# Values of the last six token tiles, two tiles at a time

## The chip, the cores and the metric

One core of a Trainium2 chip. The metric is the device time of one execution in microseconds (us); lower is better. TensorE (PE) multiplies matrices into PSUM, VectorE (DVE) and ScalarE (ACT) work on PSUM and SBUF, GpSimd (POOL) on SBUF, SyncE (SP) issues most DMAs. The engines run side by side; each takes its own instructions in the order in which they are written.

## The reference

A gated block: linear attention with a learned feature map, times a gated MLP, plus the input. There are 2048 tokens of width 640, 32 heads of 20 and a hidden width of 1536; all is float32.

```python
def _A_ref(x, wqkv, w_phi, wo):
    qkv = (x @ wqkv).reshape(B, S, 3, H, Dh).transpose(2, 0, 3, 1, 4)
    q, k, v = qkv[0], qkv[1], qkv[2]
    pq = jnp.einsum("bhsd,hdf->bhsf", q, w_phi)
    pk = jnp.einsum("bhsd,hdf->bhsf", k, w_phi)
    phi_q = jnp.concatenate([_softmax(pq), _softmax(-pq)], axis=-1)
    phi_k = jnp.concatenate([_softmax(pk), _softmax(-pk)], axis=-1)
    kv = jnp.einsum("bhsf,bhsd->bhfd", phi_k, v)
    z  = jnp.einsum("bhsf->bhf", phi_k)
    num = jnp.einsum("bhqf,bhfd->bhqd", phi_q, kv)
    den = jnp.einsum("bhqf,bhf->bhq", phi_q, z)[..., None] + 1e-6
    return (num / den).transpose(0, 2, 1, 3).reshape(B, S, D) @ wo
xn = _layernorm(x)
s = _A_ref(xn, A_wqkv, A_w_phi, A_wo)
g = _silu(_gelu(xn @ B_w1 + B_b1) @ B_w2 + B_b2)
return x + s * g
```

## The kernel before

The tokens are 16 tiles of 128; tiles 2q and 2q+1 form pair q. In the first phase each tile's normalized input, transposed and stationary, is multiplied with the weights of key, value and query (w_phi is folded into those of key and query). Every operand is split into a high and a low half, and three products of halves (`PASSES`) are summed. So `project` (L363) issues, for each of five blocks of the width, three passes of two matmuls of 128x320: 30 for one projection of one tile. Their sum lies in a PSUM bank of the pool `pA`, of which there are three.

What follows a key or a query is `feat1` and `feat2`. VectorE takes the maximum and the minimum of each head (`mx` L376, `mn` L377), subtracts the maximum (`e` L380, the last reader of the bank) and forms `nr` (L383); GpSimd makes the other half of the features from `nr` and `e` (L384, called `rest` here); ScalarE takes exp (L393). `nr` has two buffers. For a key, VectorE sums each head (L401), takes the reciprocal (L426), and GpSimd scales (`scale_heads`, L406); queries are stored to DRAM (`e_dram`) from ScalarE. `value` copies its bank into a row with ones between the heads, and two GpSimd memsets set those (L413, L414). `kv_pair` adds two tiles' products of keys and values, 64 small matmuls each, to a bank of its own.

A pair's input `xr` is prepared by `pair_stats` (mean and spread, a power on GpSimd at L231, a small store to `st_dram` and a broadcast load `bc`), `pair_sub` (GpSimd, L332), `pair_mul` (VectorE, L337) and `pair_plain` (high halves on ScalarE, L283, low halves on VectorE, L285). `t_sums` (GpSimd, five subtractions at L298) and `t_split` (ScalarE L314, GpSimd L315) make `xd`, sums of blocks of the two tiles. They serve Strassen's product in the variant with seven products: queries of pairs 4 to 7 are made by `query_pair`, both tiles at once, in seven parts of 6 or 9 matmuls, 54 for two tiles where `project` needs 60. The parts' sums, X, Y, V, Z and W, are brought together on ScalarE, GpSimd and VectorE. For this the weights' sums S1 to S4 are needed too; `fold_pair`, `s_hi` and `s_lo` make those of the query weights at tiles 4 and 5, store them to `s_dram`, and `s_back` loads them at the end. The MLP's first product uses the same `xp` and `xd`.

The order is written by hand throughout the first phase: the order of the calls in the loops over the tiles is the order on each engine. From tile 6 on a tile's step is key, value, and for tiles 6 to 9 two queries of earlier tiles; then key and value alone up to tile 15, then the four query pairs, and the MLP.

## Time and profile before

| | us |
|---|---|
| median of 3 executions | 656.03 (655.87 to 656.10) |
| the profiled execution | 655.47 |
| its span, first to last instruction | 653.8 |

The profile is of one execution, which took 655.47 us, 0.56 below the median. A share such as PE's is busy time over the span; a line such as L363 is one of the listing above. In the chain of work that ended last, each row gives start, length, engine, tile and line, and in the waits an engine's idle time is put down to what ended it. The first phase ends at about 243 us; the rest is the MLP and the attention's output.

### The profile page before, as it was taken

To read this page: it belongs to the slowest core of one execution; us is meant where nothing else is said; L and a number is where in the kernel's file an instruction comes from. 1 tells how busy PE (TensorE), PEld (TensorE's weight loads), DVE (VectorE), ACT (ScalarE), POOL (GpSimd) and SP (SyncE) were. 2 spreads that over 40 slices of the span, in tenths; PEclk is the share of its full clock that TensorE was granted. 3 is DMA by queue.
4 is the path that set the end of the run, shared out by engine and by line. 5 is a ranking of instruction groups with operands and counts; after the bars stand their busy time and mean duration, and the time that the engine had idled before them with its cause. 6 is when DMAs were issued, how large, how long until landed. Compare 5 with 4: busy or idle time off the path is not lost.

```text
span 653.8 us, 11408 instructions
## 1 busy us (share of the span) xinstructions
PE 648.0 (99%) x4414; PEld 563.0 (86%) x4414; DVE 476.0 (73%) x749; ACT 235.3 (36%) x334; POOL 389.5 (60%) x348
## 2 busy tenths in 40 slices
PE   9999999999999999999999999999999999999997
PEld 9999999999999998888888888888888886766866
DVE  6785956988655887578978967858889899852232
ACT  4512513333233357153343355742231524032130
POOL 2755464949669655867778776354462967343321
PEclk9999999999999999999999999999999999999999
DMA  9706083664204487355998899596969499989962
GB/s 351 277 1 168 12 308 133 154 181 137 84 2 162 148 286 253 121 159 203 260 257 287 230 421 290 94 335 224 171 219 259 66 270 192 301 219 260 286 228 81
DMA packets 161408, 132.22 MB, mean 202 GB/s; under 512 B 89170, under 2 KB 127314, under 8 KB 160458
## 3 DMA queue, kind: packets, MB, share of 16 engines
q1 hardware_dynamic: 158618, 119.89, 63.0%
q10 hardware_dynamic: 2736, 11.60, 4.9%
q8 instruction: 35, 0.57, 0.4%
q14 instruction: 19, 0.16, 0.1%
HBM read 83.74 MB, written 47.73 MB: 201 GB/s over the span
## 4 chain that ended last, share of the span: by engine, by line
PE 76%; DVE 3%; DMA 0%; issue 0%; POOL 0%; ACT 0%; DVEq 0%; SPq 0%; ACTq 0%
PE pB L812 24%; PE pB L783 22%; PE pB L967 11%; PE pA L363 10%; PE pA L616 4%; PE pB L914 2%; PE kv L435 1%; PE qV L616 1%; DVE y L821 1%; PE pB L921 1%; PE qY L616 1%; DMA phi_t<-eq 0%; POOL e L384 0%; DVE nr L383 0%; DVE wolh L891 0%
## 5 line engine op out<-in xcount | busy, mean ns | idle before, releaser
L812 PE MATMUL pB<-hs,w2s 128*128 128x512 f32 x720 | 165.8, 389 | 0.0
L812 PEld LDWEIGHTS pB<-hs,w2s 128*128 128x128 f32 x720 | 135.0, 188 | 28.8 <-DVE y L821 0.8
L783 PE MATMUL pB<-xp,w1s 128*128 128x512 f32 x324 | 81.4, 389 | 0.0
L783 PE MATMUL pB<-xd,w1s 128*128 128x512 f32 x324 | 79.3, 389 | 0.0
L967 PE MATMUL pB<-oT,wo 128*128 128x512 f32 (+1 forms) x315 | 72.3, 381 | 0.0
L783 PEld LDWEIGHTS pB<-xd,w1s 128*128 128x128 f32 x324 | 60.8, 188 | 12.6
L783 PEld LDWEIGHTS pB<-xp,w1s 128*128 128x128 f32 x324 | 60.7, 188 | 12.7 <-DVE pB L1048 0.2
L406 POOL TENSOR_TENSOR eq<-eq,rc 128x1280 f32<-128x1280 f32 x16 | 37.9, 2372 | 54.2 <-DVE rc L871 37.1
L967 PEld LDWEIGHTS pB<-oT,wo 128*128 128x128 f32 x315 | 57.2, 188 | 13.8 <-PE pB L914 2.5
L406 POOL TENSOR_TENSOR e<-e,rc 128x1280 f32<-128x1280 f32 x16 | 37.9, 2368 | 45.9 <-DVE rc L426 45.6
L821 DVE TENSOR_TENSOR y<-pB,y 128x512 f32<-128x512 f32 x100 | 63.1, 676 | 1.4 <-PE pB L812 1.4
L393 ACT ACTIVATE e<-e 128x1280 f32<-128x1280 f32 x32 | 40.7, 1272 | 64.4 <-POOL e L384 63.5
L788 ACT ACTIVATE pB<-pB,b1t 128x512 f32<-128x512 f32 x48 | 31.8, 662 | 78.8 <-DVE pB L1048 28.9
L363 PE MATMUL pA<-wv,xp 128*128 128x320 f32 x384 | 59.8, 310 | 0.1
L363 PE MATMUL pA<-wk,xp 128*128 128x320 f32 x384 | 59.6, 310 | 0.0
L363 PEld LDWEIGHTS pA<-wv,xp 128*128 128x128 f32 x384 | 56.9, 188 | 0.4 <-DVE e L380 0.4
L384 POOL TENSOR_TENSOR e<-nr,e 128x640 f32<-128x640 f32 x32 | 43.8, 1371 | 22.4 <-DVE nr L383 19.3
L363 PEld LDWEIGHTS pA<-wk,xp 128*128 128x128 f32 x384 | 56.9, 188 | 0.1
L858 POOL TENSOR_TENSOR ez<-eq,zrep 128x1280 f32<-128x1280 f32 x16 | 47.3, 2958 | 2.5 <-DMA eq<-e_dram 2.5
L463 POOL TENSOR_TENSOR w1s<-raw,w1s 128x640 fp32r<-128x640 f32 (+1 forms) x18 | 26.2, 1457 | 30.6 <-ACT w1s L462 30.6
L401 DVE TENSOR_REDUCE rc<-e 128x64 f32<-128x1280 f32 x16 | 23.7, 1482 | 18.4 <-ACT e L393 18.3
L970 POOL TENSOR_TENSOR xres<-gt,xres 128x256 f32<-128x256 f32 x20 | 14.3, 737 | 36.2 <-DVE gt L969 36.2
(165 smaller groups left out, 1090.2 us busy)
## 6 DMA issues: line engine op xcount, KB each, us to landing
raw<-in_w_dram SPq DMA_DIRECT2D x42, 320.0 KB
e_dram<-e ACTq DMA_DIRECT2D x16, 640.0 KB
eq<-e_dram SPq DMA_DIRECT2D x16, 640.0 KB
phi_t<-eq SPq DMA_DIRECT2D x64, 160.0 KB
phT<-phi_t SPq DMA_DIRECT2D x20, 480.0 KB
xres<-in_xt_dram SPq DMA_DIRECT2D x20, 256.0 KB
xt<-in_x_dram SPq DMA_DIRECT2D x15, 320.0 KB
out_dram<-xres SPq DMA_DIRECT2D x18, 256.0 KB
```

The source lines that it names most:

```text
L363: nc.tensor.matmul(ps[:, hf, :HALF], stat_x(q, o, k, a), ws[k][:, b, hf * HALF:(hf + 1) * HALF], start=n == 0, stop=n == 3 * KC - 1)
L384: rest = lambda: nc.gpsimd.tensor_tensor(e5[:, :, :, 1, :], nr[:, :, :, None].to_broadcast([P, 2, 16, DH]), e5[:, :, :, 0, :], op=OP.subtract)
L393: nc.scalar.activation(ef, ef, AF.Exp)
L406: nc.gpsimd.tensor_tensor(e3, e3, rc[:, :, None].to_broadcast([P, 64, DH]), op=OP.mult)
L463: nc.gpsimd.tensor_tensor(sl[:, 1, :n], src, sl[:, 0, :n].bitcast(F32), op=OP.subtract)
L616: nc.tensor.matmul(bank[ch], q_x(blk, a, q), q_weight(w, k)[:, b], start=ch not in seen and n == 0, stop=n == len(mms) - 1, skip_group_che ...
L783: nc.tensor.matmul(bank[ch][:], tl[:, a, off + wo_:off + wo_ + P], mov(blk, b), start=new and n == 0, stop=n == len(mms) - 1, skip_group_c ...
L788: nc.scalar.activation(ps, ps, AF.Gelu_apprx_tanh, bias=b1t[:, f:f + 1])
L812: nc.tensor.matmul(ps[:], ws[i][:, b, d * P:(d + 1) * P], hs[o][i][:, a, :], start=i == n == 0, stop=(i, n) == (GF - 1, 2), skip_group_che ...
L821: nc.vector.tensor_tensor(y, ps[:], y, op=OP.add)
L858: nc.gpsimd.tensor_tensor(zv, ef, zf, op=OP.mult)
L967: nc.tensor.matmul(ps[:, mv], w, o[:, mv], start=n == 0, stop=n == 15, skip_group_check=True)
```

## The change

The values of tiles 10 to 15 are no longer projected tile by tile but by pairs, with the routine of the query pairs (now `token_pair`, with the base weights and the forms handed in). The forms S1 to S4 of the value weights are made by `v_forms` from reloaded weights, for i = 0 on GpSimd at tile 5, for i = 1 on VectorE at tile 8, go through `sv_dram`, and are split by `forms` when pair 5 is at hand: high halves on ScalarE, low halves on VectorE. The query weights' sums are now stored unsplit (`sq_dram`) and split in the same way in the last pair, and the lower halves of two query slabs go through `wq_dram`. `t_sums` works in place in `xr`, and the blocks of `xd` have another order, so that `reload` has nine loads rather than eight. The steps from tile 6 to 9 prepare one pair each; then follow pairs 5 to 7, each with its two keys, a `kv_pair` and the value pair, and last the query pairs. The warm-up's ten matmuls go to one bank.

In the diff the loop that is taken out is left away; it is in the listing above.

```diff
-    s_dram = dram.tile([4, P, 2, D], F32, name="s_dram")
+    sv_dram = dram.tile([4, P, D], F32, name="sv_dram")
+    sq_dram = dram.tile([4, P, D], F32, name="sq_dram")
+    wq_dram = dram.tile([2, P, 2, HALF], F32, name="wq_dram")
...
-        return [(i, a), (2 + i, b)]
-
-    def s_hi(pairs):
-        out = []
-        for k, r in pairs:
-            hi = row([P, D], F32R, "sh")
-            nc.scalar.activation(hi[:], r[:], AF.Copy)
-            out.append((k, r, hi))
-        return out
-
-    def s_lo(parts):
-        for k, r, hi in parts:
-            nc.gpsimd.tensor_tensor(r[:].bitcast(F32R), r[:], hi[:].bitcast(F32), op=OP.subtract)
-            nc.sync.dma_start(s_dram[k][:, 0], hi[:].bitcast(F32))
-            nc.sync.dma_start(s_dram[k][:, 1], r[:])
+        nc.sync.dma_start(sq_dram[i], a[:])
+        nc.sync.dma_start(sq_dram[2 + i], b[:])
+
+    def w_dump(c):
+        nc.sync.dma_start(wq_dram[c], wq_s[c][:, :, :HALF].bitcast(F32))
+
+    def v_forms(i):
+        a, b = (load_raw(wv[c * P:(c + 1) * P, :]) for c in (i, 2 + i))
+        yield
+        eng = nc.vector if i else nc.gpsimd
+        put = lambda d, x, y, op: eng.tensor_tensor(d, x, y, op=op)
+        put(b[:, HALF:], a[:, HALF:], b[:, HALF:], OP.add)
+        put(a[:, HALF:], a[:, :HALF], a[:, HALF:], OP.subtract)
+        put(a[:, :HALF], b[:, HALF:], a[:, :HALF], OP.subtract)
+        put(b[:, :HALF], b[:, :HALF], a[:, :HALF], OP.subtract)
+        nc.sync.dma_start(sv_dram[i], a[:])
+        nc.sync.dma_start(sv_dram[2 + i], b[:])
+        yield
...
     def t_sums(q):
-        xr = xrs.pop(q)
-        tts[q] = slab(F32, "tt", (P, 9, P))
-        x_sums(lambda a, b: xr[:, a:b, :P], lambda a, b: xr[:, a:b, P:], tts[q])
+        xr = xrs[q]
+        x_sums(lambda a, b: xr[:, a:b, :P], lambda a, b: xr[:, a:b, P:],
+               lambda t: xt_two(xr.rearrange("p k (o t) -> p (k o) t", o=2), t))
 
     def t_split(q):
-        tt, dst = tts.pop(q), xd()[:, :, :, at(q)]
-        nc.scalar.activation(dst[:, :, 0, :], tt[:], AF.Copy)
-        nc.gpsimd.tensor_tensor(dst[:, :, 1, :], tt[:], dst[:, :, 0, :].bitcast(F32), op=OP.subtract)
+        dst = xd()[:, :, :, at(q)]
+        tt = xrs.pop(q).rearrange("p k (o t) -> p (k o) t", o=2)[:, :9]
+        nc.scalar.activation(dst[:, :, 0, :], tt, AF.Copy)
+        nc.gpsimd.tensor_tensor(dst[:, :, 1, :], tt, dst[:, :, 0, :].bitcast(F32), op=OP.subtract)
...
-    for pw in (bankA(), bankA()):
-        for i in range(5):
+    for pw in (bankA(),):
+        for i in range(10):
...
+    vf = [v_forms(0), v_forms(1)]
     for t in range(2, 6):
         pk = project(t, wk_s)
         if t % 2:
             kv_pair(t - 3)
         es[t] = feat1(pk)
+        if t == 4:
+            next(vf[0])
...
-            if t == 5:
-                s_lo(s_hi(srs[0]))
-            srs.append(fold_pair(t - 4))
+            fold_pair(t - 4)
+        if t == 5:
+            next(vf[0])
         feat2(es[t])
         if t == 4:
             pair_plain(3)
         phis[t] = key_fin(es.pop(t))
-        if t == 5:
-            s_lo(s_hi(srs[1]))
-    def s_back():
+    def q_back(c):
+        sl = slab(F32R, "wqb")
+        wq_b.append(sl)
+        nc.sync.dma_start(sl[:, :, :HALF].bitcast(F32), wq_dram[c])
+
+    def split_to(dst, src, eng):
+        nc.scalar.activation(dst[:, 0], src, AF.Copy)
+        eng.tensor_tensor(dst[:, 1], src, dst[:, 0].bitcast(F32), op=OP.subtract)
+
+    def forms(dram, f, base, engs):
+        raws = [load_raw(dram[k]) for k in range(4)]
+        yield
         for k in range(4):
-            sl = slab(F32R, "wqs")
-            nc.sync.dma_start(sl[:].bitcast(F32), s_dram[k])
-            wq_f.append(sl)
+            if k < 3:
+                f.append(slab(F32R, "ws"))
+            if k < 2:
+                split_to(f[k][:], raws[k][:], engs[k])
+            else:
+                split_to(base[k - 2][:, :, HALF:], raws[k][:, HALF:], engs[k])
+                split_to(f[2][:, :, (k - 2) * HALF:(k - 1) * HALF], raws[k][:, :HALF], engs[k])
+            yield
...
-    def query_pair(q, hooks, later):
+    def token_pair(q, base, f, hooks, later=None, out=None):
...
+            elif i == 2 and out:
+                nc.scalar.activation(out[0][:, 0], heads1(bank["X"]), AF.Copy)
             elif i == 3:
                 nc.vector.tensor_tensor(r2[:, 1], r2[:, 0], bank["V"], op=OP.add)
             elif i == 4:
-                nc.vector.tensor_tensor(odd[:, 1, :HALF], r2[:, 1], bank["Z"], op=OP.add)
+                o = out[1][:, 1] if out else heads1(odd[:, 1, :HALF])
+                nc.vector.tensor_tensor(o, heads1(r2[:, 1]), heads1(bank["Z"]), op=OP.add)
             elif i == 5:
-                nc.vector.tensor_tensor(bank["W"], r2[:, 1], bank["W"], op=OP.add)
-                ee = feat1(even)
+                o = out[0][:, 1] if out else heads1(bank["W"])
+                nc.vector.tensor_tensor(o, heads1(r2[:, 1]), heads1(bank["W"]), op=OP.add)
+                ee = None if out else feat1(even)
             elif i == 6:
-                nc.vector.tensor_tensor(bank["Z"], r2[:, 0], bank["Z"], op=OP.add)
+                o = out[1][:, 0] if out else heads1(bank["Z"])
+                nc.vector.tensor_tensor(o, heads1(r2[:, 0]), heads1(bank["Z"]), op=OP.add)
             if i in hooks:
                 hooks[i]()
-        return ee, feat1(odd, later)
+        return (ee, feat1(odd, later)) if not out else None
+
+    def value_pair(q, hooks):
+        vv = [value_row() for _ in range(2)]
+        token_pair(q, wv_s, wv_f, hooks, None, [v3[:, :, :DH].rearrange("p (a h) d -> p a h d", a=2) for _, v3 in vv])
+        vs[2 * q], vs[2 * q + 1] = (v for v, _ in vv)
...
+    XIN = {6: (12, 13), 8: (14, 15)}
+    STATS = {6: (10, 11), 7: (12, 13), 9: (14, 15)}
+    x_in(10)
+    x_in(11)
+    for t in range(6, 10):
+        q = t - 2
         pk = project(t, wk_s)
+        if t == 8:
+            kv_pair(6)
+        if t == 9:
+            vb = forms(sv_dram, wv_f, wv_s, [nc.vector] * 4)
+            next(vb)
+        if t == 6:
+            spill(3)
+        es[t] = feat1(pk)
+        if t > 6:
+            pair_plain(q - 1)
+        if t < 9:
+            pair_sub(q)
+        if t == 6:
+            fold_w(wqT, range(4, KC), "wq", wq_s)
+        if t < 8:
+            load_xr(q + 1)
+        feat2(es[t])
+        vs[t] = value(t)
+        phis[t] = key_fin(es.pop(t))
+        if t > 6:
+            t_sums(q - 1)
+        pq = project(next(queries), wq_s)
+        ef = feat1(pq)
+        if t < 9:
+            pair_mul(q)
+        if t in (7, 8):
+            next(vf[1])
+        for u in STATS.get(t, ()):
+            pair_stats(u)
+        store_e(queries_done.pop(0), ef)
+        pq = project(next(queries), wq_s)
+        ef = feat1(pq)
+        if t > 6:
+            t_split(q - 1)
+        store_e(queries_done.pop(0), ef)
+        if t == 6:
+            kv_pair(4)
+        if t in (6, 7):
+            w_dump(t - 6)
         for u in XIN.get(t, ()):
             x_in(u)
+    qf, later, last_sums = None, [], []
+    for p in range(5, 8):
+        t = 2 * p
+        pk = project(t, wk_s)
+        if p == 7:
+            w1r = load_w1(0)
+            qf = forms(sq_dram, wq_f, wq_b, [nc.vector] * 4)
+            next(qf)
         es[t] = feat1(pk)
+        if p == 5:
+            load_xr(7)
+            next(vb)
+            next(vb)
+        if p == 6:
+            pair_mul(7)
+        pk = project(t + 1, wk_s)
+        kv_pair(t - 2)
+        es[t + 1] = feat1(pk, later)
+        if p == 7:
+            next(qf)
+            next(qf)
+            q_back(0)
+            q_back(1)
+            wq_b.extend(wq_s[2:])
+        if p == 6:
+            pair_plain(7)
+
+        def rest(t=t, p=p):
+            later.pop(0)()
             feat2(es[t])
+            if p == 5:
+                next(vb)
+            if p == 6:
+                t_sums(7)
+            if p == 7:
+                next(qf)
+
+        def first_key(t=t, p=p):
             phis[t] = key_fin(es.pop(t))
+            feat2(es[t + 1])
+
+        def second_key(t=t, p=p):
+            if p < 7:
+                phis[t + 1] = key_fin(es.pop(t + 1))
+            else:
+                phis[t + 1] = es.pop(t + 1)
+                last_sums.append(key_sums(phis[t + 1]))
+            if p == 5:
+                pair_sub(7)
+            if p == 6:
+                t_split(7)
+
+        value_pair(p, {0: lambda: p == 5 and next(vb), 1: rest, 5: lambda: p == 7 and next(qf), 4: first_key, 6: second_key})
...
+    w1g, ea, eb = [], None, None
     for q in range(4, 8):
         if q == 7:
             w2r = [load_raw(w2[f * P:(f + 1) * P, :]) for f in range(GF)]
-        ea, eb = query_pair(q, {1: lambda: early_rest(q, ea), 3: lambda: late_rest(q, eb), **({4: last_key} if q == 4 else {})}, later)
+        hooks = {1: lambda: early_rest(q, ea), 3: lambda: late_rest(q, eb)}
         if q == 4:
-            kv_pair(NT - 4)
+            hooks[4] = last_key
+        ea, eb = token_pair(q, wq_b, wq_f, hooks, later)
```

On GpSimd before, from tile 8's two queries to the split in tile 9's step (`pst` are the statistics' powers, `tt` the sums, `e` the features, `v` the value row, `e<-nr,e` is `rest`):

```order
L384 TENSOR_TENSOR e<-nr,e 128x32x20 x2
L231 TENSOR_TENSOR pst<-pst,mhalf 128x1 x2
L384 TENSOR_TENSOR e<-nr,e 128x32x20
L298 TENSOR_TENSOR tt<-xr 128x256 x2
L298 TENSOR_TENSOR tt<-xr,tt 128x256 x2
L298 TENSOR_TENSOR tt<-xr 128x128
L413 MEMSET v 128x32
L414 MEMSET v 128x32
L406 TENSOR_TENSOR e<-e,rc 128x1280
L315 TENSOR_TENSOR xd<-tt,xd 128x9x128
```

And the same engine in tile 8's step after the change, from the key's `rest` to the split behind the queries':

```order
L392 TENSOR_TENSOR e<-nr,e 128x32x20
L340 TENSOR_TENSOR xr<-xr,bc 128x1280
L423 MEMSET v 128x32
L424 MEMSET v 128x32
L414 TENSOR_TENSOR e<-e,rc 128x1280
L301 TENSOR_TENSOR xr<-xr 128x2x128 x4
L301 TENSOR_TENSOR xr<-xr 128x128
L392 TENSOR_TENSOR e<-nr,e 128x32x20 x2
L323 TENSOR_TENSOR xd<-xr,xd 128x9x128
```

One step now holds a pair's subtraction and another's sums and split; before, tile 9's step has sums and a split only, and the next subtraction comes in tile 10's.

On ScalarE, at the beginning of pair 5's values after the change (`xd<-xr` is `t_split(6)`, the first exp is that of the last single query, stored at once, the last one that of key 10, `ws` and `wv` are high halves of the value weights' forms, `qx` the copies of X and Y):

```order
L322 ACTIVATE xd<-xr 128x9x128
L401 ACTIVATE e<-e 128x1280
L685 DMA e_dram<-e 128x1280
L609 ACTIVATE ws<-raw 128x640 x2
L657 ACTIVATE qx<-pA 128x320
L609 ACTIVATE wv<-raw 128x320
L609 ACTIVATE ws<-raw 128x320
L659 ACTIVATE qx<-qY 128x320
L401 ACTIVATE e<-e 128x1280
```

These high halves stand behind the last single query's exp and store, which before had the values' copies behind them.

On VectorE at the same place (`mx` to `nr` ahead of the forms are key 10's, those behind them key 11's):

```order
L384 TENSOR_REDUCE mx<-pA 128x32
L385 TENSOR_REDUCE mn<-pA 128x32
L388 TENSOR_TENSOR e<-pA,mx 128x32x20
L391 TENSOR_TENSOR nr<-mn,mx 128x32
L610 TENSOR_TENSOR ws<-raw,ws 128x640 x2
L384 TENSOR_REDUCE mx<-pA 128x32
L385 TENSOR_REDUCE mn<-pA 128x32
L388 TENSOR_TENSOR e<-pA,mx 128x32x20
L391 TENSOR_TENSOR nr<-mn,mx 128x32
L610 TENSOR_TENSOR wv<-raw,wv 128x320
L610 TENSOR_TENSOR ws<-raw,ws 128x320
```

The two low halves that Y reads come between the two keys; those of S1 and S4 come behind key 11.

More of the change, by code (lines that the diff above doesn't have):

```diff
@@ L185, in fold_w @@
         return mm, lo
-    srs = []
     def fold_pair(i):
@@ L615, in query_pair @@
             for n, (w, k, b, blk, a) in enumerate(mms):
-                nc.tensor.matmul(bank[ch], q_x(blk, a, q), q_weight(w, k)[:, b], start=ch not in seen and n == 0,
+                nc.tensor.matmul(bank[ch], q_x(blk, a, q), p_weight(base, f, w, k)[:, b], start=ch not in seen and n == 0,
                                  stop=n == len(mms) - 1, skip_group_check=True)
@@ L674, in hedgehog_gated_mlp_kernel @@
-        if t == 13:
-            w1r = load_w1(0)
-        if t in (7, 9, 11, 13):
-            t_sums((t + 1) // 2)
-        if t == NT - 1:
-            s_back()
-        vs[t] = value(t)
-        if t < NT - 1:
-            feat2(es[t])
-        if t in (8, 10, 12):
-            pair_plain(q)
-        if t < NT - 1:
-            phis[t] = key_fin(es.pop(t))
-        if t in (7, 9):
-            t_split((t + 1) // 2)
-        if t == 6:
-            query(next(queries))
-            query(next(queries))
-            pair_plain(4)
```

99 lines of the change are left out of this document (42 added, 57 removed).

## The prediction

> **What bounds the kernel now.** I read the busy shares first, then TensorE's own waits, then the chain that ended last, then the time line of the stretch that is changed.
>
> ```profile
> PE 648.0 (99%) x4414; PEld 563.0 (86%) x4414; DVE 476.0 (73%) x749; ACT 235.3 (36%) x334; POOL 389.5 (60%) x348
> ...
> PE pA L499 <- PEq L1213: 0.8, 1, 0.8
> PE pA L363 <- DVE e L380: 0.6, 1, 0.6
> PE pB L921 <- DVE y L821: 0.4, 1, 0.4
> ...
> 136.98 0.76 DVE mx L376
> 137.74 0.72 DVE mn L377
> 138.46 0.74 DVE e L380
> 139.20 0.14 issue
> 139.34 22.23 PE pA L363 x150
> 161.57 1.32 PE kv L435 x125
> ...
> 182.02 26.60 PE pA L363 x180
> ...
> 139.34 1.99 PE L363 MATMUL pA<-wv,b 128*128 128x320 f32 x12 [0.56 <-DVE e L380]
> ```
>
> TensorE is busy for 648.0 of 653.8 us and waits three times, for 1.8 us in all (second piece: the waits of TensorE, with their sum, count and longest). So a matmul that goes is time that goes, as long as no wait comes in its place. The chain (third piece: start, length, engine) shows the one wait in the changed stretch: TensorE starts at 139.34, 0.56 late (last row, of the time line), when VectorE (DVE) has read a bank with `mx`, `mn` and `e` that the next projection wants. Everything else that the change touches lies off TensorE, so the question is what the other engines still have to do, and by when.
>
> **What is removed.** The values of tiles 10 to 15 are six projections of 30 matmuls in before, three pairs of 54 in after: 18 matmuls of 128x320 less. The chain has 180 of them in 26.60 us, 148 ns each: **-2.66 us**. If the wait at 139 goes too, 0.56 more: the multiply and the plain split that make VectorE late ahead of it are another pair's now and stand elsewhere, so I take it as gone. **-3.2** with nothing new. The ten warm-up matmuls go to one bank instead of two: 0.
>
> **What is added and moved off TensorE.** The weights' forms cost VectorE, ScalarE and GpSimd (POOL) work, and `pair_sub`, `t_sums` and `t_split` of pairs 5 and 6 move into tiles 7 to 9, where before had about half as many. The prices:
>
> ```profile
> L384 POOL TENSOR_TENSOR e<-nr,e x32: 1270/1277/2540, 22.1 to 247.9; 128x640 f32<-128x640 f32 x32
> L406 POOL TENSOR_TENSOR e<-e,rc x16: 2367/2368/2373, 31.0 to 216.6; 128x1280 f32<-128x1280 f32 x16
> L332 POOL TENSOR_TENSOR xr<-xr,bc x5: 2952/3005/3009, 61.1 to 180.3; 128x1280 f32<-128x1280 f32 x5
> L298 POOL TENSOR_TENSOR tt<-xr x12: 462/736/752, 113.7 to 199.8; 128x256 f32<-128x256 f32 x8, 128x128 f32<-128x128 f32 x4
> L315 POOL TENSOR_TENSOR xd<-tt,xd x4: 2679/2681/2690, 119.7 to 203.9; 128x1152 fp32r<-128x1152 f32 x4
> L231 POOL TENSOR_TENSOR pst<-pst,mhalf x10: 549/550/556, 49.7 to 144.5; 128x1 f32<-128x1 f32 x10
> L413 POOL MEMSET v<- x16: 159/166/188, 30.2 to 211.3; 128x32 f32 x16
> L337 DVE TENSOR_TENSOR xr<-xr,bc x5: 1492/1494/2550, 64.1 to 183.3; 128x1280 f32<-128x1280 f32 x5
> L285 DVE TENSOR_TENSOR xp<-xr,xp x10: 551/684/827, 68.9 to 187.8; 128x640 fp32r<-128x640 f32 x5, 128x384 fp32r<-128x384 f32 x5
> L285 DVE TENSOR_TENSOR b<-xr,b x5: 416/418/419, 69.7 to 187.4; 128x256 fp32r<-128x256 f32 x5
> L383 DVE TENSOR_TENSOR nr<-mn,mx x32: 175/508/2840, 20.9 to 247.6; 128x32 f32<-128x32 f32 x32
> L393 ACT ACTIVATE e<-e x32: 1255/1274/1278, 23.9 to 249.4; 128x1280 f32<-128x1280 f32 x32
> L145 ACT ACTIVATE wv<-raw x5: 720/724/741, 16.0 to 21.7; 128x640 fp32r<-128x640 f32 x5
> L147 DVE TENSOR_TENSOR wv<-raw,wv x1: 812/812/812, 21.9 to 21.9; 128x640 fp32r<-128x640 f32 x1
> ...
> 159.20 3.00 POOL L332 TENSOR_TENSOR xr<-xr,bc 128x1280 f32<-128x1280 f32 x1
> 159.34 0.33 ACTq L420 DMA_DIRECT2D e_dram<-e  x1
> 159.41 2.84 DVE L383 TENSOR_TENSOR nr<-mn,mx 128x32 f32<-128x32 f32 x1
> 162.24 1.49 DVE L337 TENSOR_TENSOR xr<-xr,bc 128x1280 f32<-128x1280 f32 x1
> 162.33 2.54 POOL L384 TENSOR_TENSOR e<-nr,e 128x640 f32<-128x640 f32 x1
> ...
> 115.13 1.49 DVE L401 TENSOR_REDUCE rc<-e 128x64 f32<-128x1280 f32 x1 [2.75 <-ACT e L393]
> 115.15 1.57 POOL L298 TENSOR_TENSOR tt<-xr,tt 128x256 f32<-128x256 f32 x2
> ```
>
> (A group's row: least, median and longest ns, and from when to when; a row of the time line: start and length.) The two pieces of time line decide. `nr`, a subtraction of 32 columns that takes 0.18 us with nothing in its way, began at 159.41, while GpSimd's subtraction ran (159.20 to 162.20), and ended with it, at 162.25. Then the roles turn: `rest` (L384) began at 162.33 behind VectorE's multiply and took 2.54 instead of 1.28, its own time and the rest of the multiply's. The reduction, which has one input, ran its usual 1.49 beside GpSimd. So here a VectorE instruction with two inputs from SBUF and one of GpSimd run one after the other, and their times add up, whatever each engine's own share. The Trainium skill, "SBUF — State Buffer", section "SBUF: two separate sides", says as much of the port pair of the two, "an exclusive lock, not a bandwidth split" held for a whole instruction, and the trace agrees; by that page's rule this change puts work of just the kind that contends beside GpSimd's, and without it the sum would be that of the first rival.
>
> So I count the two together, from the end of key 7 to `rest` of the eighth query (query 7), since the first forms of the values wait behind that one.
>
> ```profile
> 101.49 1.92 PE L363 MATMUL pA<-wv,b 128*128 128x320 f32 x12
> ...
> 101.50:162.40 60.90, 60.20 (x618) 59.26 (x617) 47.54 (x83) 21.89 (x23) 42.60 (x40) 1.00 0.49 142
> ...
> 110.11 0.55 POOL L231 TENSOR_TENSOR pst<-pst,mhalf 128x1 f32<-128x1 f32 x1 [5.50 <-DVE pst L233]
> 183.35 2.55 DVE L337 TENSOR_TENSOR xr<-xr,bc 128x1280 f32<-128x1280 f32 x1 [2.94 <-POOL xr L332]
> ```
>
> Key 7's matmuls end at 101.5 (the value's begin), and nothing ahead of them gets slower. GpSimd then has nine `rest` 11.5, three scalings (L406) 7.1, two `pair_sub` 6.0, three `t_sums` of 4 x 0.74 + 0.46 10.3, two `t_split` 5.4, four powers 2.2, six memsets 1.0: 43.5 us. VectorE has with two inputs: three `pair_plain` of 0.82 + 0.42 + 0.55 5.4, two multiplies 3.0, nine `nr` 1.6, four operations of `v_forms(1)` at half of the 0.81 of L147, as they have half its columns, 1.6: 11.6. Together 55.1. Before, GpSimd is busy 42.6 us of these 60.9 (windows: us, then busy time of PE, PEld, DVE, ACT, POOL, the clock, DMA share and GB/s).
>
> `rest` of key 7 can begin 2.2 us after its projection (`mx`, `mn`, `e`), at 103.7, so query 7's ends at 158.8 at the earliest, with no gap on either engine. In-order queues have gaps (GpSimd waited 5.50 for a power at 110); I take half of that, 2.7, so **161.5**, bounds 158.8 and 163.
>
> When is it wanted? The `kv` at 161.57 stands behind 13 projections since key 7, in after too (key 11 in the place of value 10). So pair 5's value begins at 161.57 + 1.32 - 0.56 = 162.3, and its second part, Y, six matmuls later at 163.2; Y is the first to want the forms. On ScalarE their high halves stand behind exp of query 7 (1.27) and the issue of its store (0.33): the first is there at 161.5 + 1.6 + 0.72 = 163.8, the second 0.7 later. The low halves (0.81 each) are VectorE's, again with two inputs, against `t_split(6)`, which follows `rest` on GpSimd at once, to 164.2. So 165.0 for the first, 165.8 for the second, or 167.1 if `rest` of key 10 gets in between. Y wants them at 163.35 and 163.8. **2.0 to 3.3 us of stall; I take 2.6**, bounds 0 (at 160.0 and before) and 4.5 (at 163).
>
> Behind these splits stands key 11's `mx`, `mn`, `e` (2.2), then the low halves of S1 and S4 (four of 0.41). S1 is read from 30 matmuls after pair 5's start, 4.4 us: its two halves are wanted at 162.3 + 2.6 + 4.4 = 169.3 and 169.8. They are ready at 165.8 + 2.4 + 0.8 = 169.0 and, behind exp of key 10 on ScalarE and `rest` of key 11 on GpSimd, 1.5 to 2.5 later. **0 to 2.0; I take 1.4**, since one GpSimd instruction is nearly sure to be in the way. In pair 6, `pair_sub(7)` comes behind both scalings on GpSimd: pair 5 ends at 162.3 + 4.0 + 8.0 = 174.3, then a reduction and its reciprocal (2.0), a scaling and the subtraction: 181.7; its multiply ends at 183.2 or, as at 183.35 in the row, 1.06 later, where key 13's bank is full at 174.3 + 8.9. So VectorE is 0 to 1.1 late there, and the copies of X behind `pair_plain` with it. **0 to 1.7 with one more GpSimd instruction's half; I take 0.6**, nearest to the free multiply.
>
> Costed at nothing: the splits of the query forms in the last pair (2 x 0.81 + 4 x 0.41), under five projections' time and with GpSimd's sums done; uncovered, up to 1.6. The dropped splits of tile 5 and `v_forms(0)` lie long before, on no path. The stores and reloads go through SyncE's queue, issued some 20 us ahead of use; the ninth reload ahead of the FFN has the slack of the other eight, on whose data no wait of TensorE falls.
>
> The sum, in the profiled execution's own time (655.47 us, span 653.8): -3.2 + 2.6 + 1.4 + 0.6 = +1.4, so 656.9. That execution lies 0.56 below the median of before, so **657.4** beside 656.03.
>
> **Rivals.** (1) *The cover holds*: gaps are filled and the low halves get through at once. Y waits 0 to 1, S1 not, pair 6 0 to 0.3: from -3.2 to -1.9, 652.8 to 654.1. For it: GpSimd starts the stretch with nothing left over. Against: Y's halves are in time only if `rest` ends by 160.0 (exp, store, two high halves and a low one, 3.85 us, back from 163.8), which leaves 1.2 us of gaps in a stretch of 55. (2) *The stall eats the gain*: Y 2.0, S1 0.7, pair 6 0.3: -3.2 + 3.0, about no change, 655.8. (3) *The lock costs more*, the slower side: `rest` of query 7 at 163, because each VectorE instruction of this kind that comes behind a GpSimd one of 1.28 to 3.00 also delays VectorE's queue, whose `nr` GpSimd then waits for. Every us beyond 160 passes to Y nearly one for one; the change loses from a stall of 3.2 us in all, at about 160.8; at 163 it is 4.5 + 2.0 + 1.7, so 661.0. My forecast is its mild part. (4) *A reload is late*: the forms' four loads stand in SyncE's queue behind waits for the small stores, 4.1 us each:
>
> ```profile
> SPq L326 <- DMA st_dram<-pst: 20.5, 5, 5.1
> ```
>
> Three such waits in a row and they come 12 us later, with some 20 to spare. Worth up to 4 us; a small chance.
>
> **How the numbers follow.** About 0.2% (1.3 us) is what a measurement of this kernel can tell from no change. A stall below 1.9 us in all (under 654.7, faster): rival 1, 0.30. Between 1.9 and 4.5 (to 657.3, the same): rival 2 and the lower end of the forecast, 0.28. Above (slower): the rest of the forecast, rivals 3 and 4, 0.42. The forecast's own range is 656 to 659, as cases of both signs hold most of the chance. The range for 8 in 10 takes in nearly all of rival 1 and of rival 3: 653.0 to 660.6.
>
> **What would show it.** In the changed profile: 18 matmuls fewer in the first phase, at 148 ns; `rest` of query 7 ending at 161 to 162; a TensorE wait of 2 to 3 us at pair 5's Y for VectorE's low halves, and a smaller one at its S1 part; `nr` and the splits at two or more times their free length, each ending with a GpSimd row. I am wrong if `rest` of query 7 ends by 159, if those splits take 0.81, or if TensorE waits elsewhere, at a key's bank in tiles 8 or 9, where VectorE's own lag would show first.

## The result and the profile after

The changed kernel takes 663.78 us (663.49 to 664.84, 4 runs), the one before 655.95 beside it (655.81 to 656.10): a ratio of 1.0122, with a 95% interval of 1.0105 to 1.0140. It is 7.8 us slower, where 1.4 were forecast, and lies above the range (653.0 to 660.6). The profiled execution took 663.49 us, its span is 661.4.

First the busy shares and the waits of TensorE in the changed kernel (in us: sum, count, longest), then its stretches around the longest wait (from and to, length, busy time of PE, PEld, DVE, ACT and POOL; the granted clock stands third from the right):

```profile
PE 648.8 (98%) x4396; PEld 562.4 (85%) x4396; DVE 501.6 (76%) x777; ACT 237.4 (36%) x345; POOL 395.5 (60%) x351
...
PE qY L653 <- ACT ws L609: 2.6, 1, 2.6
PE pA L371 <- DVE nr L391: 2.0, 1, 2.0
PE qY L653 <- DVE ws L610: 1.1, 2, 0.6
PE pA L653 <- DVE pA L667: 1.0, 1, 1.0
...
143.00:145.20 2.20, 0.20 (x2) 0.03 (x1) 2.20 (x5) 0.08 (x1) 2.09 (x3) 1.00 0.93 298
166.10:168.60 2.50, 0.00 (x0) 0.00 (x0) 0.00 (x0) 2.02 (x4) 2.21 (x1) 0.96 1.06 102
168.60:175.00 6.40, 5.25 (x17) 4.51 (x18) 6.35 (x8) 4.11 (x10) 4.32 (x8) 0.50 0.94 222
175.00:176.00 1.00, 1.00 (x8) 1.00 (x7) 1.00 (x2) 0.83 (x2) 0.47 (x1) 0.89 1.13 348
```

The 18 matmuls are gone (4396 instead of 4414), yet TensorE is busy 0.8 us longer: its clock is halved for some 6.8 us, from the end of the longest wait on (0.96 over 2.5 us is 0.2 at half, 0.89 over one another 0.2), which makes the same work longer by 648.8 - (648.0 - 2.7) = 3.5 us. The balance of the spans, 661.4 - 653.8 = 7.6, closes: -2.7 for the matmuls, -0.6 for the wait at 139 us, +6.7 for the four waits shown, +0.7 for two small ones (0.4 at the start, 0.3), +3.5 for the clock.

The time line shows how the longest wait comes about (start and length, and in brackets the idle time before and what ended it):

```profile
110.25 2.99 POOL L340 TENSOR_TENSOR xr<-xr,bc 128x1280 f32<-128x1280 f32 x1 [3.86 <-issue]
132.92 2.99 POOL L340 TENSOR_TENSOR xr<-xr,bc 128x1280 f32<-128x1280 f32 x1 [3.67 <-DMA wq_dram<-wq]
135.99 3.67 POOL L414 TENSOR_TENSOR e<-e,rc 128x1280 f32<-128x1280 f32 x1
137.35 5.51 DVE L214 TENSOR_TENSOR raw<-raw 128x320 f32<-128x320 f32 x4
139.62 4.24 POOL L301 TENSOR_TENSOR xr<-xr 128x256 f32<-128x256 f32 x5
...
156.18 2.37 POOL L414 TENSOR_TENSOR e<-e,rc 128x1280 f32<-128x1280 f32 x1 [3.43 <-DVE rc L441]
158.50 3.63 POOL L301 TENSOR_TENSOR xr<-xr 128x256 f32<-128x256 f32 x5
162.09 1.28 POOL L392 TENSOR_TENSOR e<-nr,e 128x640 f32<-128x640 f32 x1
164.36 1.28 POOL L392 TENSOR_TENSOR e<-nr,e 128x640 f32<-128x640 f32 x1
166.15 1.25 ACT L401 ACTIVATE e<-e 128x1280 f32<-128x1280 f32 x1
167.88 1.36 ACT L609 ACTIVATE ws<-raw 128x640 fp32r<-128x640 f32 x2 [0.48 <-ACT e L401]
168.65 2.85 DVE L610 TENSOR_TENSOR ws<-raw,ws 128x640 fp32r<-128x640 f32 x2 [2.90 <-ACT ws L609]
168.67 0.64 PE L653 MATMUL qY<-ws,xd 128*128 128x320 f32 x1 [2.64 <-ACT ws L609]
```

GpSimd stands still three times: in tiles 7 and 8 at `pair_sub` (L340), whose broadcast of the statistics comes late, and in tile 9 at the key's scaling (L414), for the key's sums. The pair's sums (L301), which need neither, stand behind. The rows of the two waits at `pair_sub` do not name the broadcast (`bc`). For the first, the chain that ended last leads to it through the store of the statistics and the load `bc` (start, length). And the row of e4 below, where the same two waits occur, names the load:

```profile
98.77 7.57 DMA st_dram<-pst
106.35 0.03 DMA bc<-st_dram
106.39 3.86 issue
110.25 0.07 POOL xr L340
...
POOL xr L340 <- DMA bc<-st_dram: 6.4, 2, 3.5
```

So `rest` of queries 6 and 7 (the two L392) end at 163.4 and 165.6, the exp follows, and the first high half of Y's forms is ready when TensorE has waited 2.6 us; the second low half ends at 171.5. Between the second and the third standstill, `v_forms(1)` takes VectorE 5.5 us for four operations, and the scaling and the sums of GpSimd beside it 3.7 and 4.2 where they take 2.4 and 3.6 in tile 9: that is the wait of 2.0 us at 143 us, where the first query of tile 9 wants the bank of the last query of tile 8.

### The profile page after: what moved, and what is told of

Its sections match the earlier page's. It is cut to its first block, busy times and chain, and to the rows that moved or that the text cites. A ratio compares the mean times of both kernels' runs of the same rounds, so it can differ in the third digit from the quotient of the medians.

```text
span 661.4 us, 11452 instructions
## 1 busy us (share of the span) xinstructions
PE 648.8 (98%) x4396; PEld 562.4 (85%) x4396; DVE 501.6 (76%) x777; ACT 237.4 (36%) x345; POOL 395.5 (60%) x351
## 4 chain that ended last, share of the span: by engine, by line
PE 81%; DVE 5%; DMA 5%; POOL 4%; issue 2%; SPq 1%; ACT 1%; ACTq 0%; DVEq 0%; POOLq 0%
PE pB L909 24%; PE pB L880 22%; PE pA L371 11%; PE pB L1067 11%; PE pA L653 5%; DMA st_dram<-pst 2%; PE pB L1014 2%; PE pA L174 1%; POOL xr L301 1%; PE qV L653 1%; PE kv L453 1%; DMA folds<-in_wqk_dram 1%; POOL e L414 1%; POOL e L392 1%; PE qY L653 1%
## 5 line engine op out<-in xcount | busy, mean ns | idle before, releaser
L909 PE MATMUL pB<-hs,w2s 128*128 128x512 f32 x720 | 165.8, 389 | 0.0
L414 POOL TENSOR_TENSOR eq<-eq,rc 128x1280 f32<-128x1280 f32 x16 | 37.9, 2370 | 55.9 <-DVE rc L971 38.7
L392 POOL TENSOR_TENSOR e<-nr,e 128x640 f32<-128x640 f32 x32 | 46.4, 1449 | 23.5 <-DVE nr L391 18.0
L414 POOL TENSOR_TENSOR e<-e,rc 128x1280 f32<-128x1280 f32 x16 | 39.2, 2450 | 35.0 <-DVE rc L441 35.0
L371 PE MATMUL pA<-wv,xp 128*128 128x320 f32 x240 | 37.7, 311 | 0.0
L371 PEld LDWEIGHTS pA<-wv,xp 128*128 128x128 f32 x240 | 35.5, 188 | 0.1
L891 DVE TENSOR_TENSOR hs<-pB,hs 128x512 fp32r<-128x512 f32 x48 | 32.0, 683 | 3.9 <-ACT hs L887 3.7
```

What stands on the lines that cost most here:

```text
L371: nc.tensor.matmul(ps[:, hf, :HALF], stat_x(q, o, k, a), ws[k][:, b, hf * HALF:(hf + 1) * HALF], start=n == 0, stop=n == 3 * KC - 1)
L392: rest = lambda: nc.gpsimd.tensor_tensor(e5[:, :, :, 1, :], nr[:, :, :, None].to_broadcast([P, 2, 16, DH]), e5[:, :, :, 0, :], op=OP.subtract)
L414: nc.gpsimd.tensor_tensor(e3, e3, rc[:, :, None].to_broadcast([P, 64, DH]), op=OP.mult)
L891: nc.vector.tensor_tensor(hs[:, 1], ps, hs[:, 0].bitcast(F32), op=OP.subtract)
L909: nc.tensor.matmul(ps[:], ws[i][:, b, d * P:(d + 1) * P], hs[o][i][:, a, :], start=i == n == 0, stop=(i, n) == (GF - 1, 2), skip_group_che ...
```

## Experiments

Each is an edit of the changed kernel. The ratio is to the runs of the kernel before that stood beside it.

| run | us | ratio (95%) |
|---|---|---|
| changed kernel | 663.78 | 1.0122 (1.0105 to 1.0140) |
| e1_sub_late | 660.72 | 1.0076 (1.0061 to 1.0091) |
| e2_no_sums | 662.86 | 1.0106 (1.0091 to 1.0121) |
| e3_fill_y | 661.84 | 1.0096 (1.0081 to 1.0111) |
| e4_order_only | 656.84 | 1.0020 (1.0009 to 1.0031) |
| e5_split_early | 661.65 | 1.0091 (1.0075 to 1.0107) |
| e6_fill_all | 663.03 | 1.0113 (1.0097 to 1.0128) |
| e7_one_input | 663.08 | 1.0117 (1.0101 to 1.0132) |
| e8_combined | 659.85 | 1.0061 (1.0045 to 1.0078) |
| e9_sums_first | 660.20 | 1.0066 (1.0051 to 1.0081) |
| e10_three | 659.21 | 1.0051 (1.0034 to 1.0068) |
| e11_stats_early | 664.03 | 1.0124 (1.0109 to 1.0140) |
| e12_two_pairs | 665.40 | 1.0150 (1.0133 to 1.0167) |
| e13_all_early | 657.44 | 1.0031 (1.0019 to 1.0043) |
| e14_all_early_tiles | 655.02 | 0.9992 (0.9983 to 1.0000) |

**The order or the product (e4).** The values by tile, in the new order:

```diff
-        value_pair(p, {0: ..., 1: rest, 5: ..., 4: first_key, 6: second_key})
+        rest()
+        vs[t] = value(t)
+        first_key()
...
+        vs[t + 1] = value(t + 1)
+        second_key()
```

> The changed kernel's order of work, but with the values of tiles 10 to 15 projected tile by tile and without the value forms (no v_forms, no splits of them). If the loss sits in the wait for the forms: no wait of TensorE over 1 us is left, PE's busy time is that of before, 655.5 to 657 us. If the order itself costs (the late broadcast holds up GpSimd, and the keys' banks come free late): waits of 2 us or more at L371 remain, 658 to 661 us.

656.84, the first case: 1.0 us over the kernel before, with one new wait of TensorE over 0.3 us:

```profile
PE pA L371 <- ACT v L430: 0.9, 1, 0.9
```

So 6.9 of the 7.8 us come with the product in pairs and its forms, 18 matmuls less notwithstanding; the order by itself is nearly free. GpSimd waits for the broadcast in this run too (6.4 us, the row above), so that wait costs little where no forms hang on it.

**The lock (e2, e7).** Without the four operations of `v_forms(1)` (e2), and with operations of the same size and one input in their place (e7):

```diff
-        put(b[:, HALF:], a[:, HALF:], b[:, HALF:], OP.add)
...
+            for d, x in ((b[:, HALF:], a[:, HALF:]), ...):
+                nc.vector.tensor_reduce(d, x[:, :, None], axis=AX.X, op=OP.max)
```

> The changed kernel without the four VectorE operations of v_forms(1) in tile 8 (the sums of the value weights' blocks 1 and 3 are left out, the blocks themselves are stored in their place); nothing else. Theory B (lock): in the profile these four take 5.5 us together beside GpSimd's scaling and sums, which take 3.7 and 4.2 us instead of 2.4 and 3.4; without them the 2.0 us wait at a query's bank at 143 us goes, and GpSimd's row is about 2 us earlier there: 661 to 662 us, and less still if the wait at Y gets shorter. Theory A alone (only the late broadcast counts): the wait at the bank goes, as VectorE has less to do, but Y comes 2 us earlier while its forms do not: its wait grows to about 4.5, 663 to 664.5 us.

> The changed kernel with the four VectorE operations of v_forms(1) replaced by reductions over one element, of the same 128x320 out but with one input (what they compute is no longer the forms). If two inputs from SBUF are what GpSimd's work shuts out: the four take about 1.9 us together instead of 5.5, GpSimd's scaling beside them 2.4 instead of 3.7, and the time is that without the four, 662.5 to 663. If any VectorE work on SBUF contends, or the four wait for one another: 5 us or more, and 663.8.

The time line of e7 at that place:

```profile
136.66 3.68 POOL L419 TENSOR_TENSOR e<-e,rc 128x1280 f32<-128x1280 f32 x1
138.03 1.91 DVE L223 TENSOR_REDUCE raw<-raw 128x320 f32<-128x320 f32 x4
140.30 3.63 POOL L306 TENSOR_TENSOR xr<-xr 128x256 f32<-128x256 f32 x5
```

Four operations with one input take 1.91 us beside GpSimd's scaling, as expected (about 1.9), and those with two inputs 5.51; the sums behind take 3.63 instead of 4.24. (The scaling stays at 3.68: the multiply of `pair_mul` ahead, also with two inputs, holds it up.) This shows the lock. It does not show much of the time: both runs are within 1 us of the changed kernel, with overlapping intervals. The wait of 2.0 us became one of 2.4 to 2.8 a projection later, for ScalarE's copy of a value, which stands behind an exp that waits for a late `rest`. My expectation of e2 (661 to 662) failed in this.

**Where the splits stand (e5).** The two splits for Y moved ahead of query 6's exp, into tile 9:

```diff
-            next(vb)
-            next(vb)
...
+        if t == 9:
+            next(vb)
+            next(vb)
```

> The changed kernel with the splits of the two forms that Y reads moved from behind key 10 to tile 9, behind the first query's reading of its bank: their high halves then stand on ScalarE in front of that query's exp rather than behind exp and store of both. Theory D (Y waits because these splits stand behind the exps of queries 6 and 7, whose `rest` GpSimd makes late; where they stand decides): the waits at Y (2.6 and 1.1) go, TensorE never stands still for more than 2.0 us, the clock stays at 1.00 and with it the 3.5 us of longer matmuls go; the wait of 2.0 at 143 us stays, and up to 1.5 us may come at S1: 656.5 to 658.5 us. Rival (VectorE and GpSimd have too much to do there, wherever it stands): the two splits hold up query 6's and key 10's banks instead, a wait of 2 us or more at L371 after 150 us, 660 to 663 us.

661.65: the time of the rival, but not its wait of 2 us or more. Y no longer waits and the clock stays at 1.00, but the wait at 143 us stays (1.7), and TensorE waits 1.6 us for the copy of X, 1.5 for S1's low halves and 1.2 for a bank instead. The copy of X stands in ScalarE's queue behind the same exp of query 7. So Y's forms were only the first to show that GpSimd, and all that hangs on it, is late.

**GpSimd's idle times (e1, e9).** First `pair_sub` moved behind the first query, and `pair_mul` behind the second (e1); then, from the changed kernel again, `t_sums` moved directly behind `pair_plain`, ahead of `pair_sub` and the scaling (e9):

```diff
-        if t < 9:
-            pair_sub(q)
...
         ef = feat1(pq)
         if t < 9:
-            pair_mul(q)
+            pair_sub(q)
...
         ef = feat1(pq)
+        if t < 9:
+            pair_mul(q)
```

```diff
             pair_plain(q - 1)
+            t_sums(q - 1)
...
-        if t > 6:
-            t_sums(q - 1)
```

> The changed kernel with pair_sub moved behind the first query of its step and pair_mul behind the second; nothing else. Theory A (GpSimd stands still at pair_sub of pairs 5 and 6, 3.9 and 3.7 us, because the broadcast of the statistics is not there yet, and this lag reaches the value forms): the two idle times go, `rest` of query 7 ends 3 to 6 us earlier than 165.6, the 2.6 us wait at Y falls below 1, the granted clock stays at 1.00, 656 to 659 us. Theory B (the lag is the sum of VectorE's and GpSimd's two-input work, as I had forecast; the idle times only take the place of waits for the lock): GpSimd's waits move elsewhere, `rest` of query 7 gains at most 1 us, 662 to 664 us.

> The changed kernel with t_sums moved to directly behind pair_plain, ahead of pair_sub and of the key's scaling; nothing else. Theory E (GpSimd, which takes its work in order, is late because it stands still at pair_sub for the broadcast, 3.9 and 3.7 us in tiles 7 and 8, and at the scaling for the key's sums, 3.4 us in tile 9, while the sums, which need neither, stand behind): the sums, 3.6 us each, fill most of these gaps, `rest` of query 7 ends 3 to 5 us earlier than 165.6, the wait at Y falls to under 1 us, the clock stays at 1.00, the 2.0 us at 143 us shrink or go: 656.5 to 659 us. If GpSimd's gaps are not what sets Y (VectorE's own lag, or the lock): 662 to 664 us, the gaps only move.

The idle times of GpSimd from 101.5 to 165 us, of the changed kernel and then of e9:

```profile
POOL e L392 <- DVE nr L391: 4.8, 3, 2.8
POOL xr L340 <- issue: 3.9, 1, 3.9
POOL xr L340 <- DMA wq_dram<-wq: 3.7, 1, 3.7
POOL e L414 <- DVE rc L441: 3.4, 1, 3.4
POOL xd L323 <- ACT xd L322: 2.2, 2, 1.6
```

```profile
POOL e L392 <- DVE nr L391: 13.7, 6, 3.8
POOL pst L234 <- DVE pst L236: 0.7, 1, 0.7
POOL xr L340 <- issue: 0.7, 1, 0.7
```

In e9 GpSimd's waits for the broadcast and for the key's sums are gone but for 0.7 us, as expected, and Y no longer waits for the high halves; it gains 3.6 us. But GpSimd now waits 13.7 us for `nr`, that is, for VectorE, and TensorE 1.8 for a bank and 1.4 for Y's low halves: the lag has moved over to VectorE. In e1 the wait at `pair_sub` went as well, and VectorE's multiply waited 3.0 us for it instead; Y still waited 2.3. `rest` of query 7 ends 2.1 us earlier in e1 and 1.6 in e9, where 3 to 6 and 3 to 5 were expected. Both gained 3 to 3.6 us and both stopped short of what their theory gave. Not all of e9's gain is GpSimd's: its clock is halved for 3.4 us (last section) instead of 6.8.

**Three at once, and on (e8, e10, e11, e13).** e8 has e1's and e5's moves and `v_forms(1)` on GpSimd in tile 5 (first diff); e10 has e9's instead of e1's; e11 is e10 with the inputs loaded and reduced earlier (second diff); e13 is e10 with the third:

```diff
-        eng = nc.vector if i else nc.gpsimd
+        eng = nc.gpsimd
...
             next(vf[0])
+            next(vf[1])
...
-        if t in (7, 8):
-            next(vf[1])
```

```diff
             x_in(10)
+            x_in(11)
...
         pk = project(t, wk_s)
+        for u in XIN.get(t, ()):
+            x_in(u)
...
+        for u in STATS.get(t, ()):
+            pair_stats(u)
         feat2(es[t])
         vs[t] = value(t)
```

```diff
-        for u in STATS.get(t, ()):
-            pair_stats(u)
+        if t < 9:
+            for u in STATS.get(t, ()):
+                pair_stats(u)
...
         ef = feat1(pq)
+        if t == 9:
+            for u in STATS[t]:
+                pair_stats(u)
...
-        value_pair(p, {0: lambda: p == 5 and next(vb), 1: rest, 5: lambda: p == 7 and next(qf), 4: first_key, 6: second_key})
+        value_pair(p, {1: rest, 4: first_key, 6: second_key})
```

In the third the splits taken out of the hooks stand behind key 10 and in `rest`.

> The changed kernel with three moves at once: the two splits for Y in tile 9 (as in the run of that name), pair_sub and pair_mul behind the queries of their step, and v_forms(1) on GpSimd in tile 5, behind v_forms(0), where GpSimd had idle time. If the loss is all order: the waits at 143 us and at Y go, the 18 matmuls saved come through but for 1 to 1.5 us at S1 and pair 6: 653.5 to 655.5 us, at or below the kernel before. If the product in pairs costs by itself what it saves: 656 to 658 us.

> The run with the sums first, with Y's two splits in tile 9 and v_forms(1) on GpSimd in tile 5 besides. Theory E with the lock: no wait of TensorE over 1 us between 100 and 180 us, clock 1.00, and what the product in pairs saves comes through but for 1 us: 653.5 to 655.5 us, at or below the kernel before. If something else holds the copies of X and Y (ScalarE's queue, where they stand behind query 7's exp): 1.5 to 3 us remain there, 656 to 658.5 us.

> The run with these three, and the inputs and statistics of tiles 10 to 15 half a step to a step earlier, so that the broadcast is there when pair_sub wants it. If the late broadcast still counts: 0.5 to 2 us below the run with three (GpSimd's idle time at pair_sub gone). If the sums already cover it: the same within 0.5 us.

> The run with three, with three further moves: the statistics of tiles 14 and 15 behind the second query of tile 9 rather than between the two (2.6 us of VectorE ahead of query 7's bank), the splits for S1 and S4 of the values directly behind key 10, and the last split of the query forms one hook earlier. If what is left of the loss is VectorE and ScalarE work standing ahead of what TensorE waits for: the waits for X's copy (1.0), S1's low halves (1.5) and in the first query pair (1.1) go, 655.5 to 657 us. If they are taken over by others, because VectorE and GpSimd together have no more room there: 658 to 660 us.

e8 and e10 missed both of their cases: 659.85 and 659.21. In e10 GpSimd no longer waits at `pair_sub` at all, so there was nothing left for e11 to take away; its first phase is no better, and a new wait of 4.5 us, which ends with the last query's `nr`, stands at the start of the MLP. e13 comes to 657.44, between its two cases and the best with pairs; the wait for X's copy stays, S1's is down to 0.3, and a new one of 1.8 has come in pair 5, for VectorE's reading of a bank. Its waits of TensorE between 100 and 250 us, and behind them those of e14:

```profile
PE pA L655 <- DVE v L669: 2.0, 2, 1.8
PE pA L655 <- ACT qx L659: 1.0, 1, 1.0
...
PE pA L655 <- DVE wv L612: 0.3, 1, 0.3
```

```profile
PE pA L517 <- PEq L1307: 0.8, 1, 0.8
PE pB L1015 <- DVE y L912: 0.4, 1, 0.4
```

**The worth of the product (e14).** e13's order with the values by tile:

> The same order as in the run before it, with the values of tiles 10 to 15 projected tile by tile and none of their forms. Against that run it tells what the product in pairs is worth by itself: its 18 matmuls are 2.7 us. If the pairs give all of it once nothing is late: 2 to 3 us above that run, 656 to 658.5 us. If the forms take back what the matmuls save: equal to it or faster.

655.02, 0.8 us below the kernel before (0.9992, to 1.0000: just at the edge of what can be told) and 2.4 below e13: the other way from what I expected. Only the start's and the output's small waits are left in it (last fence). In this order the pairs save 2.7 us of matmuls and cost 5.1 in waits and the rest. In e13 VectorE is busy for 15.6 of the 17.1 us from 162.9 to 180, in e14 for 10.1 (columns as in the stretches of the changed kernel):

```profile
162.90:180.00 17.10, 14.02 (x93) 13.23 (x92) 15.56 (x23) 5.08 (x9) 11.72 (x12) 1.00 0.59 170
162.90:180.00 17.10, 17.10 (x119) 17.05 (x117) 10.06 (x13) 4.17 (x5) 12.18 (x10) 1.00 0.56 170
```

**Two pairs only (e12).** With pair 5's values by tile:

```diff
+        if p == 5:
+            rest()
+            vs[t] = value(t)
+            first_key()
+            vs[t + 1] = value(t + 1)
+            second_key()
+            continue
```

> The changed kernel with the values of pair 5 projected tile by tile, and those of pairs 6 and 7 in pairs; the forms for S1 and S4 are split in pair 6. If all of the loss sits at pair 5, where the forms come too early behind the late queries: the order's own 1.0 us and the bank wait of 2.0 us at 143 us stay, 12 matmuls (1.8 us) are saved: 656 to 658 us, no wait at a Y, clock 1.00. If each pair costs more than it saves: 659 us or more, with waits at pairs 6 and 7.

665.40, the slowest of all: the second case, with waits in pair 6, though not in pair 7.

```profile
PE pA L653 <- ACT qx L657: 2.4, 1, 2.4
PE pA L653 <- DVE wv L610: 2.3, 2, 1.2
```

The wait of 2.4 us is for X's copy and the one of 2.3 for S1's low halves, now in pair 6: there all of the forms' second half and pair 7's multiply and plain split come together. So pair 5 is not the only place without room.

**The clock (e3, e6).** Matmuls that need nothing late, put into Y's waits (e3; in e6 there are 6 and 5 more behind Y's first and fourth, and all go to the bank that Z starts afresh):

```diff
+            if out and q == 5 and i == 1:
+                for _ in range(17):
+                    nc.tensor.matmul(bank[ch], q_x(0, 0, q), p_weight(base, f, "A11", 0)[:, 0], start=True, stop=True)
```

> The changed kernel with 17 more matmuls of 128x320 (2.5 us) at the head of Y of pair 5, into Y's own bank, which Y then starts afresh; they need nothing that is late and so fall into the 2.6 us wait. Theory C (the granted clock falls to 0.50 for about 7 us because TensorE stood still for 2.6 us, and the 3.5 us of longer matmuls are all lost): clock 1.00 throughout, 660 to 661 us. Rival: VectorE's low halves of S1 are late anyway, so faster matmuls only wait there: clock 1.00, a new wait of 1 to 2 us at the part with S1, 662.5 to 663.5 us. Should the clock fall all the same: unchanged, 663.8 us.

> The changed kernel with 28 more matmuls in the waits of pair 5's Y (17 at its head, 6 and 5 behind its first and fourth matmul, into the bank that Z later starts afresh), so that TensorE has work throughout. If the clock is set by how long TensorE has stood still: 1.00 throughout. What is then left tells what the fall of the clock cost: 3.5 us less than the changed kernel (660.3) if the longer matmuls are all lost time; 661 to 662 if half of them only shorten the wait for S1's low halves behind. With 17 at the head the time was 661.84, and the clock still fell, for 3.2 us.

The stretches around Y in e3, and the one from 160 to 180 in e6 (the same columns):

```profile
165.00:168.70 3.70, 3.68 (x35) 3.38 (x23) 0.90 (x3) 3.02 (x4) 2.96 (x2) 1.00 0.91 147
168.70:171.90 3.20, 1.28 (x5) 0.79 (x6) 3.12 (x3) 1.71 (x5) 2.55 (x6) 0.98 0.96 277
171.90:175.10 3.20, 3.20 (x13) 3.20 (x14) 3.20 (x6) 2.35 (x5) 1.80 (x2) 0.50 0.93 208
...
160.00:180.00 20.00, 18.70 (x241) 17.57 (x240) 16.92 (x29) 9.93 (x14) 12.98 (x16) 1.00 0.66 162
```

With the head filled the clock holds to about 171.8 and then falls for some 3.4 us, after two waits on low halves (1.8 us in sum); with those filled too (e6) it stays at 1.00 from 160 to 180. So here it fell behind a TensorE without work, and not where the waits were filled. The gain is 1.9 us in e3, between its first two cases, and 0.8 in e6 (28 matmuls, which are 0.4 us longer than the waits they fill), whose 663.03 lies above both of its own. It is not 3.5: neither interval reaches 1.007, which 3.5 us less would be. Y ends when the low halves are there, and in e6 S1's low halves then kept TensorE waiting for 0.8 us, so a part of the 3.5 us stood in time that would have been waited.

The profile of e3 is of the longest of its four executions: 663.56 us at a mean granted clock of 0.996. The others took 661.37 to 662.00 at 1.000; 3.4 us at half would take 0.003 off that mean. So the fall does not come in every execution of the same kernel, and where it came, behind Y, it went with about 1.9 us, one execution against three.

## Why the prediction was wrong

The forecast added 1.4 us, the spans 7.6. Between them stand the longer matmuls (3.5), the bank wait (2.0), the first query pair (1.0) and two small waits (0.7), none of which had a term; the stalls that had one came to 3.7 instead of 4.6. These are the places where time was lost, not yet its causes: e2 took the bank wait away and gained 0.9 us, since TensorE waited elsewhere instead. What TensorE waits for up to Y is VectorE's and GpSimd's work, and that was late by more than forecast.

- **18 matmuls, -2.7 us; the wait at 139 us, -0.6.** Right, both.
- **Lock of VectorE and GpSimd.** The mechanism was right (e7: 1.91 against 5.51 us), the sum too strict. From 103.7 to 165.6 us the rows of GpSimd and of VectorE's operations with two inputs from SBUF (L214, L288, L345, L391) cover 50.1 us, 5.0 less than the 55.1 of the forecast, so a part of them did run side by side.
- **"I take half of that, 2.7".** This is the step that failed. For 11.9 of these 61.9 us neither engine was at such work, where 2.7 were taken. With the 5.0 off, `rest` of query 7 ended at 165.6 instead of 161.5, and the second low half at 171.5 instead of 165.8. 8.4 of the 11.9 us lie in three waits of GpSimd: for the broadcast (3.9 and 3.7) and for the key's sums (3.4). I had costed GpSimd's instructions by length and not by place. The sums, which before stood ahead of the scaling, stand behind it now, so GpSimd waits with work of its own behind; the order rows ahead of the prediction show it. e9 shows that these gaps can be filled, though GpSimd then waits for VectorE instead. The bound of 163 was too low for the same reason.
- **Y, 2.6 us (0 to 4.5); S1 1.4; pair 6 0.6.** Y's waits were 2.6 and 1.1, 3.7 in sum and within the bounds, but by luck: the forms were later than forecast by 4.8 to 5.7 us, and TensorE came to Y 2.8 us later, having waited before. S1 and pair 6 waited for nothing; where Y's wait was taken away (e5, e10), S1's came, with 1.5, which fits that Y had already waited for them.
- **No bank wait.** The text named a wait at a key's bank in tiles 8 or 9 as what would prove it wrong, and nearly that is what came: 2.0 us at 143, at a query's bank in tile 9, from the locked `v_forms(1)` and a multiply behind the late `pair_sub`. It had no term.
- **"Costed at nothing: the splits of the query forms".** The first query pair waited 1.0 us, within the 1.6 named for the case without cover.
- **The matmuls' length.** I priced every matmul at 148 ns. Behind the long wait 3.5 us were added by a halved clock, which no row of before could show; filling the waits gave back 1.9 (e3) and 0.8 (e6).
- **Rival 3**, the lock costing more, was the right direction. Its stalls at Y, S1 and pair 6 were too large (8.2, measured 3.7), and its 661.0 still too low, since the bank wait, the query pair, the small waits and the clock were not in it. Rival 4 had the right queue and the wrong load: the broadcast was late, not the forms' loads.

What stays open: e2, e5, e9 and e12 each moved a lag rather than took it away. That VectorE and GpSimd together are short of room from tile 7 to pair 6 fits all of these and e14, but it is argued and not shown: no run shows how much of either's work would have to go before the pairs pay. Why the MLP waited for the last query in e11 was not tried either.

## What to carry to other kernels

On an engine that takes its work in order, price an instruction by what it waits for and what stands behind it, not by its length: work that needs nothing late belongs ahead of the instruction that waits. When matmuls are bought with arithmetic on engines that already lag, compare with the same order without the purchase (e13 against e14), since taking one wait away shows the next. And a wait of TensorE can cost more than its length, so a forecast that adds a wait of 2 us needs a term for the clock.

## What the hardware showed that I had not expected

A wait of under 2 us can halve the granted clock, and a longer one may not. The windows of e9 behind its wait of 1.84 us (143.5 to 145.3):

```profile
145.00:146.00 1.00, 0.68 (x5) 0.71 (x6) 1.00 (x4) 0.00 (x0) 0.65 (x1) 1.00 1.14 351
146.00:147.00 1.00, 1.00 (x7) 1.00 (x7) 1.00 (x3) 0.34 (x1) 1.00 (x2) 0.74 0.89 182
147.00:148.00 1.00, 1.00 (x6) 1.00 (x5) 1.00 (x2) 0.93 (x1) 1.00 (x1) 0.50 0.93 295
...
149.00:150.00 1.00, 1.00 (x5) 1.00 (x5) 0.99 (x2) 0.99 (x3) 0.87 (x2) 0.56 1.07 416
150.00:151.00 1.00, 1.00 (x9) 1.00 (x8) 1.00 (x2) 0.00 (x0) 1.00 (x1) 1.00 1.02 358
```

It fell to 0.50 about 1.2 us after TensorE had work again (0.74 from 146 to 147), for 3.4 us. In the changed kernel the wait of 2.0 us at the same place left it at 1.00, and that of 2.6 at Y brought 6.8 us at 0.50. The Trainium skill, "TensorE: Matmul & The Clock Gate", section "Part 1: The HAM clock gate", gives windows of about 3.4 us that run freely, and half the clock after an idle one. The lengths agree (3.4, and 6.8 is two of them), and so does the chance in it: a 1.84 us wait that brings the fall and a 2.0 us wait that doesn't, and e3's four executions, of which one shows it. But neither 1.84 nor 2.6 us is as long as a window, so here a window that was idle only in part was enough.
